# Splitting a parameter load, folding gates into small vectors and shifting with a second tensor, in a long convolution with a gated feed-forward

## The chip, the cores and the metric

The kernel runs on one core of a Trainium2 chip. The metric is the device time of one execution in microseconds, and less is better. The core's engines each work through a queue of their own in order: TensorE (PE in the profile, PEld for its weight loads), VectorE (DVE), ScalarE (ACT), GpSimd (POOL) and SyncE (SP), which issues most DMAs. TensorE writes to PSUM, which this kernel uses as eight banks of 128 x 512 float32. A "column" below is one element in each of 128 partitions.

## The reference

With L = 2048 tokens, D = 640 channels, N = 128 states per channel and F = 1728:

```python
mod = (silu(c) @ w_mod).reshape(1, 6, 1, 640)
sa, ca, ga, sb, cb, gb = (mod[:, i] for i in range(6))
h = layernorm(x) * (1 + ca) + sa
x = x + ga * A(h)
h = layernorm(x) * (1 + cb) + sb
x = x + gb * B(h)

# A(u): a long convolution, channel by channel
dt = exp(log_dt); A = -exp(log_A_real) + 1j * A_imag
C = (C_real + 1j * C_imag) * dt[:, None]
K[d, l] = 2 * Re(sum over n of C[d, n] * exp(A[d, n] * dt[d] * l))
y = irfft(rfft(u, 4096) * rfft(K, 4096))[:2048] + u * D_skip

# B(x): a gated feed-forward
out = (silu(x @ w1) * (x @ w3)) @ w2
```

All is float32.

## The kernel before, in words

The program has two parts. The first, up to about 376 us of the span, is A with the first layer norm; the second is B. The change is in the first.

**Blocks and chunks.** A goes through the 640 channels in five blocks of 128 (b = 0 to 4). The kernel K of a block is generated in eight chunks of 16 channels (`gen_chunk`): POOL adds two tables of phases into `ph` (`g*.ph` in the plan) and multiplies two tables of magnitudes into `yy` and `xx` (`z0` to `z2`), ScalarE takes sines of `ph` into PSUM (`s0` to `s4`, tile `tr`), VectorE multiplies them with the magnitudes (`m0` to `m4`), PE contracts over the states into `kps` (`p`), and ScalarE copies the result into `ks` (`r`). The tokens of the block go another way: they are normalized into a PSUM bank (`h*.n`, tile `hn`), multiplied by the row `rA` (`h*.x`), `rB` is added (`h*.a`, tile `hb`), and they go through DRAM into `xb`. Both then pass a two-stage Fourier transform on PE (tiles `ps`, then `fh` and `fk`), a product on VectorE (`fp`), an inverse stage (`fz`) and a store (`zd`).

**Tables.** For each half block, `tables` makes the phase tables `p1` (eight entries) and `p2` (four) from a start `pB` and a step `pS`, which are integers whose overflow is the wrap of the angle. Doublings of the step (times 1, 2, 4, 8, 16) are made first, then sums fill the tables. For the first half of block 0 VectorE makes the doublings by five shifts; for the other nine POOL makes them by a copy and four additions of a number to itself (tiles `p` and `step`).

**Gates.** `row` makes the first three rows of mod on PE; ScalarE copies them into `m`, PE spreads them over the partitions (`prow`), ScalarE copies them into `rows`, and `fold` on VectorE makes rA = (1 + ca) ga and rB = sa ga, 640 columns each. So the gate ga is applied to the tokens ahead of the convolution.

**Parameters.** The four parameter arrays of all blocks are loaded as 128 x 640, one DMA each, ahead of the tokens `xs`. `param_steps` then works on them: the turning angles for all five blocks at once (`pa`), the magnitudes and angles of C for block 0 and for the rest apart (`pb`, `pc`), and PE turns the results so that states lie on partitions (`ptp`).

**Order.** The 1,507 tasks of this part are added to a `Plan` with engines and dependencies, and they are issued in the order that the table `ORDER` gives; a letter behind a number chooses the engine where there are two (`a` ScalarE, `d` VectorE, `p` POOL). Each engine keeps that order. A wait at the head of a queue thus holds up all behind it. Nearly all instructions are recorded under one helper line (L146 before, L147 after), so the tile's name tells them apart.

**PSUM.** Three banks are for `tr`, one for `kps`, and four for everything else. `pbank` hands these four out in turn: three in a ring with the tag `f`, and each fourth request gets the one with the tag `x`. Some early tasks take only from the ring.

Of the kernel before, what the change touches and what calls it, by code (L numbers as in the profile page):

```python
# [10 lines left out]
F32 = mybir.dt.float32  # L11
F32R = mybir.dt.float32r
I32 = mybir.dt.int32
# [5 lines left out]
P = 128  # L19
# [9 lines left out]

EXPS = ((0, 0, 0, 64.0), (0, 1, 0, 1.0), (1, 0, 0, 512.0), (1, 1, 4, 8.0), (1, 2, 0, 8.0))  # L30
# [4 lines left out]
1 2 3 78 4 80 5 6 81 19 14 82 20 41 84 21 7 15 83 42 8 22 153d 9 13 16 154 43 17 23 10 44 24 18 93 25 28 45 89 59 30 26 29 46 31  # L35
35 91 39 47 27 48 87 96 49 36 100 33 156 61 98 50 109 37 157 34 60 107 32 158 105 111 51 102 113 95 52 88 104 90 53 62 108 72 74
70 76 38 40 159p 160 155d 85 161 103 162 114 116 54 115 170 55 174 117 186 97 118 94 119 171 79 112 86 120 56 99 172 57 121 175
179 187 176 313 58 177 180 173 64 106 182 190 188 11 67 298 181 178 189 191 183 122 66 192 196 308 65 193 202 197 195 194 184 68
110 303 199 63 101 123 206 203 69 71 92 138 419d 207 12 185 124 208 140 198 205 142 127 204 125 200 209 163 128 420 218 132 166d
213 164 144 212 221 211 421d 214 165 167 219 168 169 75 73 77 126 134 135 129 130 133 139 210 314d 222 131 309a 227 141 136 304a  # L40
215 234 310 216 315 223 311 224 220 143 316 312 217 237 305 299a 339 228 422 306 229 335 307 225 146 226 317 238 145 231 235 201
300 336a 250 239 230 337 240 245 232 241 301 236 242 243 302 233 251 148d 247 341 244 254 253 338d 255 246 252 256 147 266 342a
260 248 149 259 257 318 261 150 258 425d 262 267 249 270 343 340a 269 151 263 271 275 268 264 272 277 282 276 273 265 278 274
345 344a 426 279 286 283 287 346a 423 291 288 284 427 424 285 428 152 0 564 569 319 565d 321 320a 289 333 570a 292 579 566 280
294 334a 322a 829 567 436 327 290 293 281 571 331 328a 295 440 437 137 580d 347 441 439 332a 442 572 296 574 438 447 443 452 445
325 444 581 297 348a 568 446 329 326a 449 455 456 448 349 457 453 458 463 450 684p 350d 330a 830d 459 323 451 460 454 582 834
# [1849 lines left out]
```

## Time and profile before

| | us |
|---|---|
| median of three runs | 946.7 |
| lowest, highest | 944.83, 949.02 |
| profiled execution, its own time | 945.42 |
| its span, first to last instruction | 943.6 |

The mean granted clock of TensorE was 0.986. Over the whole span PE is busy for 848.8 us (90%), VectorE for 699.6 (74%), ScalarE for 524.2 (56%), POOL for 341.3 (36%). These shares mix two parts with different limits, so tables by stage are read instead. A row of a group gives engine, operation, output<-inputs, shape and count, then busy time, mean duration of one in ns, and the idle time of the engine just before. In a timeline the columns are start, length, engine, operation and, in brackets, idle time and what ended it. A row of waits gives who waited for whom, the total, how often, and the longest.

### The profile page before, as it was taken

To read this page: it belongs to the slowest core of one execution; us is meant where nothing else is said; L and a number is where in the kernel's file an instruction comes from. 1 tells how busy PE (TensorE), PEld (TensorE's weight loads), DVE (VectorE), ACT (ScalarE), POOL (GpSimd) and SP (SyncE) were. 2 spreads that over 40 slices of the span, in tenths; PEclk is the share of its full clock that TensorE was granted. 3 is DMA by queue.
4 is the path that set the end of the run, shared out by engine and by line. 5 is a ranking of instruction groups with operands and counts; after the bars stand their busy time and mean duration, and the time that the engine had idled before them with its cause. 6 is when DMAs were issued, how large, how long until landed. Compare 5 with 4: busy or idle time off the path is not lost.

```text
span 943.6 us, 21995 instructions
## 1 busy us (share of the span) xinstructions
PE 848.8 (90%) x8963; PEld 671.7 (71%) x8963; DVE 699.6 (74%) x1223; ACT 524.2 (56%) x900; POOL 341.3 (36%) x352
## 2 busy tenths in 40 slices
PE   1167788989989997999999999999999999999997
PEld 0035767767868752777877788888888888888875
DVE  7999999989999855467567576467568777765763
ACT  6898999989788842333333244344344434445331
POOL 1888999988999533000000000001133322200000
PEclk9998999999999997999999999999999999999999
DMA  9776554433223468965515262322132111123242
GB/s 210 236 255 166 169 139 121 105 103 92 59 71 89 130 187 238 235 176 158 157 55 150 84 166 79 112 84 71 36 79 81 51 44 48 41 83 112 74 152 82
DMA packets 124940, 112.77 MB, mean 120 GB/s; under 512 B 12328, under 2 KB 107048, under 8 KB 123560
## 3 DMA queue, kind: packets, MB, share of 16 engines
q1 hardware_dynamic: 124072, 110.46, 42.1%
q8 instruction: 70, 1.15, 0.5%
q10 hardware_dynamic: 768, 0.92, 0.4%
q14 instruction: 30, 0.25, 0.1%
HBM read 90.38 MB, written 20.97 MB: 118 GB/s over the span
## 4 chain that ended last, share of the span: by engine, by line
PE 65%; DVE 17%; ACT 7%; DMA 6%; issue 3%; POOL 1%; SPq 1%; DVEq 0%; ACTq 0%; POOLq 0%
PE p L819 17%; PE acc L1066 17%; PE gu L1029 7%; PE gu L1031 6%; PE gu L1030 6%; DVE yy L146 5%; DVE fp L146 3%; DVE xx L146 2%; DMA xs<-in_x 2%; ACT tr L146 2%; PE fz L146 2%; PE kps L146 2%; PE ps L146 2%; DVE fk L146 1%; PE fk L146 1%
## 5 line engine op out<-in xcount | busy, mean ns | idle before, releaser
L1029 PE MATMUL gu<-xh,wh 128*128 128x512 f32 x270 | 106.1, 398 | 1.6 <-ACT xh L608 1.4
L1031 PE MATMUL gu<-xh,wl 128*128 128x512 f32 x270 | 105.4, 390 | 0.0
L1030 PE MATMUL gu<-xl,wh 128*128 128x512 f32 x270 | 105.2, 389 | 0.0
L146 ACT ACTIVATE tr<-ph 128x512 f32<-128x512 int32 (+1 forms) x160 | 93.6, 601 | 11.4 <-DVE yy L146 6.9
L838 POOL TENSOR_TENSOR ws<-wp 128x256 f32<-128x256 f32 x13 | 9.6, 739 | 230.9 <-DVE x L609 116.0
L146 POOL TENSOR_TENSOR ph<-p,p 128x1024 int32<-128x1024 int32 x40 | 79.1, 1979 | 11.4 <-ACT tr L146 8.6
L146 DVE TENSOR_TENSOR yy<-yy,tr 128x512 f32<-128x512 f32 (+1 forms) x80 | 75.1, 942 | 1.1
L722 ACT ACTIVATE wh<-wr 128x640 fp32r<-128x640 f32 x51 | 35.0, 732 | 67.8 <-PE gu L1030 58.3
L819 PE MATMUL p<-x,wch 128*128 128x512 f32 x208 | 68.3, 389 | 0.0
L1029 PEld LDWEIGHTS gu<-xh,wh 128*128 128x128 f32 x270 | 50.6, 188 | 17.6 <-DVE al L609 2.1
L1031 PEld LDWEIGHTS gu<-xh,wl 128*128 128x128 f32 x270 | 50.7, 188 | 11.2 <-DVE wl L732 0.4
L146 PE MATMUL kps<-yy,xx 128*32 128x64 f32 x2560 | 48.7, 226 | 10.9 <-DVE xx L146 6.4
L1030 PEld LDWEIGHTS gu<-xl,wh 128*128 128x128 f32 x270 | 50.7, 188 | 10.2 <-DVE xl L609 0.2
L735 POOL MEMSET w2l<- 64x640 f32 x1 | 0.6, 627 | 157.1 <-PE acc L1066 157.1
L146 DVE TENSOR_TENSOR xx<-tr,xx 128x512 f32<-128x512 f32 x80 | 54.2, 679 | 1.2 <-ACT tr L146 0.7
L856 DVE TENSOR_TENSOR s<-p,s 128x512 f32<-128x512 f32 x52 | 34.7, 683 | 26.8 <-ACT s L854 22.8
L146 POOL TENSOR_TENSOR yy<-e,e 128x512 f32<-128x512 f32 x48 | 52.9, 1110 | 3.3 <-issue 1.7
L1042 ACT ACTIVATE th<-gu 128x512 f32<-128x512 f32 x26 | 15.6, 600 | 65.7 <-PE gu L1031 65.7
L146 PE MATMUL ps<-wk,xb 128*64 128x128 f32 x640 | 47.7, 297 | 4.9 <-DVE hb L146 1.9
L1044 DVE TENSOR_TENSOR a<-a,gu 128x512 f32<-128x512 f32 x26 | 17.9, 687 | 45.4 <-PE gu L1031 45.2
L146 PEld LDWEIGHTS kps<-yy,xx 128*32 128x32 f32 x2560 | 42.9, 112 | 11.7 <-issue 8.5
L146 PEld LDWEIGHTS ps<-wk,xb 128*64 128x64 f32 x640 | 42.9, 220 | 10.4 <-DVE hb L146 2.2
(378 smaller groups left out, 2378.9 us busy)
## 6 DMA issues: line engine op xcount, KB each, us to landing
wr<-in_w SPq DMA_DIRECT2D x52, 320.0 KB, 3.6
zd<-zt SPq DMA_DIRECT2D x39, 256.0 KB, 4.1
w2r<-in_w SPq DMA_DIRECT2D x26, 320.0 KB, 3.5
wp<-in_w SPq DMA_DIRECT2D x26, 320.0 KB, 3.6
wq<-in_w SPq DMA_DIRECT2D x26, 320.0 KB, 3.3
low<-zd SPq DMA_DIRECT2D x48, 160.0 KB, 5.5
xs<-in_x SPq DMA_DIRECT2D x16, 320.0 KB, 11.3
hs<-hb SPq DMA_DIRECT2D x20, 256.0 KB, 3.1
```

The lines of the kernel that those rows point to most:

```text
L146: self.prev = self.k.order(f(*a, **kw), self.prev)
L722: self.nc.scalar.activation(wh[:, i], raw[:, i], AF.Copy)
L735: self.nc.gpsimd.memset(w2l[64:].bitcast(F32), 0.0)
L819: nc.tensor.matmul(to, t[:, o], y[:, k], start=start and k == i == 0, stop=stop and (k, i) == (n - 1, 2), skip_group_check=True)
L838: G.tensor_tensor(s[0], a21, a22, op=ALU.add)
L856: add = lambda o, bk, s: V.tensor_tensor(o, bk, s, op=ALU.add)
L1029: nc.tensor.matmul(pg, wh[:, k, :], xh[:, k, :], start=(k == 0), stop=False)
L1030: nc.tensor.matmul(pg, wh[:, k, :], xl[:, k, :], start=False, stop=False)
L1031: nc.tensor.matmul(pg, wl[:, k, :], xh[:, k, :], start=False, stop=(k == KT - 1))
L1042: nc.scalar.activation(th, gu[0], AF.Tanh, scale=0.5)
L1044: nc.vector.tensor_mul(a, a, gu[1])
L1066: nc.tensor.matmul(acc[k], *two(a, w), start=(m == 0 and i == 0), stop=(m == 12 and i == 2))
```

## The change

Five edits come at once, with a new `ORDER` of 1,500 tasks.

1. Loads. Block 0's parameters are loaded first by four DMAs of 128 x 128, the rest behind by four of 128 x 512. The turning angles, the exponential of log_A and its product with dt are worked for block 0 and for the rest apart.
2. Gates. The rows of mod are turned onto partitions by PE into a bank (`vp`), and eight small VectorE instructions (`vc`) make A = (1 + ca) ga and B = sa / (1 + ca) there, with block 0's B multiplied by its A. PE spreads A and B over the partitions. Only block 0's tokens are still multiplied by rA. For blocks 1 to 4 A goes into the magnitudes of K (`gm`, four POOL instructions) and into D_skip (`gd`, four), and `h*.x` is gone.
3. Tables. For every half block VectorE makes all five doublings in one `tensor_tensor` shift of 128 x 640, whose second input is a tensor of amounts. POOL keeps four sums per table.
4. Banks. The four banks have names. In running the order, `Plan.run` gives each request the bank whose last release stands earliest in the order.
5. The tiles `ph`, `xx` and `yy` are allocated by their own tasks, and the magnitudes (`z`) no longer follow `ph` in the plan.

```diff
+SHIFTS = 0, 1, 3, 2, 4
...
-        def begin(e):
-            by = by_t(pS)
-            to = (p1[:, :, :, 1], by_t(st[:, 0]), by_t(st[:, 1]), p2[:, :, :, 1], by_t(st[:, 2]))
-            for i, d in enumerate(to):
-                if e == "DVE":
-                    V.tensor_scalar(d, by, i, None, op0=ALU.logical_shift_left)
-                elif i:
-                    add(d, to[i - 1], to[i - 1])
-                else:
-                    G.tensor_copy(d, by)
+        def begin():
+            sh = self.shifts
+            amounts = bass.AP(tensor=sh.tensor, offset=sh.offset, ap=[list(sh.ap[0]), [0, HB2], [0, 2], list(sh.ap[1])])
+            V.tensor_tensor(p1[:, :, :, 1:6], bc(by_t(pS), 3, 5), amounts, op=ALU.logical_shift_left)
...
+        def bank(key):
+            free = [-1 if k is None else max((at.get(x, 1e9) for x in self.gives.get(k, [])), default=1e9) for k in held]
+            i = free.index(min(free))
+            held[i] = key
+            return i
...
     def pbank(self, name):
-        self.banks += 1
-        if self.banks % 4 == 3:
-            return self.psx.tile([P, 512], F32, name=name, tag="x")
-        return self.psg.tile([P, 512], F32, name=name, tag="f", bufs=3)
+        return self.psg.tile([P, 512], F32, name=name, tag=f"b{self.plan.banks.pop(0)}", bufs=1)
...
-            add(n + "x", "DVE", .61, lambda i=i: self.h_mul(b, i), [n + "n", "fold"], t + .1)
+            if b == 0:
+                add(n + "x", "DVE", .61, lambda i=i: self.h_mul(b, i), [n + "n"] + rows, t + .1)
...
-        add("T", "SP", 0, lambda: self.param_load(T, slice(0, NB)), [], next(lp), dma=[327680] * 3)
+        add("T0", "SP", 0, lambda: self.param_load(T, one), [], next(lp), dma=[65536] * 3)
+        def load_rest():
+            nc.sync.dma_start(self.la[:, 1:], self.log_ar.rearrange("(k p) n -> p k n", p=P)[:, 1:])
+            self.param_load(T, rest)
...
+        def gates():
+            pv = mt[1]
+            sa, ca, ga = (pv[:, k * KT:k * KT + KT] for k in range(3))
+            z, A, B, q = pv[:, 16:16 + KT], ab[:, :KT], ab[:, KT:2 * KT], ab[:, 2 * KT:]
+            V.tensor_scalar(q, ca, 1.0, None, op0=ALU.add)
+            V.scalar_tensor_tensor(z, q, -1.0, q, op0=ALU.mult, op1=ALU.max)
+            V.tensor_scalar(z, z, 1e-18, 4e-18, op0=ALU.is_lt, op1=ALU.mult)
+            V.tensor_tensor(q, z, q, op=ALU.add)
+            V.tensor_mul(A, q, ga)
+            V.reciprocal(q, q)
+            V.tensor_mul(B, sa, q)
+            V.tensor_mul(B[:, :1], B[:, :1], A[:, :1])
...
-        def fold():
-            self.rA, self.rB = self.rows[1], self.rows[0]
-            V.scalar_tensor_tensor(self.rA, self.rA, 1.0, self.rows[2], op0=ALU.add, op1=ALU.mult)
-            V.tensor_mul(self.rB, self.rB, self.rows[2])
+        def gate_sizes(e):
+            m = self.mag[:, 1:].rearrange("p b (e j) -> p b e j", j=4)
+            r = self.rA[:, P:].rearrange("p (b j e) -> p b e j", j=4, e=E4)
+            for k in range(NB - 1):
+                self.eng(e).tensor_tensor(m[:, k], m[:, k], r[:, k], op=ALU.mult)
```

Where instructions moved is seen best at three places. The first is the start of VectorE's queue, behind the instructions on dt (`st_n`); `wb` holds exp(log_A), `x_e` the imaginary parts and C, `xb` and `ks` scratch. Before:

```order
L146 TENSOR_TENSOR wb<-wb,st_n_95 128x640
L146 TENSOR_TENSOR x_e<-x_e,st_n_95 128x640
L146 TENSOR_TENSOR xb<-x_e 128x128
L146 TENSOR_SCALAR ks_134<-x_e 128x640
L146 TENSOR_SCALAR xb<-xb 128x128
L146 TENSOR_TENSOR ks_133<-al,j_109 128x1024
```

Now:

```order
L147 TENSOR_TENSOR xb<-x_e 128x128
L147 TENSOR_TENSOR x_e<-x_e,st_n_92 128x128
L147 TENSOR_SCALAR xb<-xb 128x128
L147 TENSOR_SCALAR ks_136<-x_e 128x128
L147 TENSOR_TENSOR wb<-wb,st_n_92 128x128
L147 RECIPROCAL xb<-xb 128x128
L147 TENSOR_TENSOR ks_135<-al,j_106 128x1024
L147 TENSOR_TENSOR x_e<-x_e,st_n_92 128x512
```

Seven instructions on block 0 now stand ahead of the first one that needs the rest of the parameters.

The second place is the table of the second half of block 2. On POOL before (`p_123` is `p1`, `p_124` is `p2`):

```order
L146 COPY p_123<-pS 128x128
L146 TENSOR_TENSOR step<-p_123 128x64x2
L146 TENSOR_TENSOR step<-step 128x64x2
L146 TENSOR_TENSOR p_124<-step 128x128
L146 TENSOR_TENSOR step<-p_124 128x64x2
L146 TENSOR_TENSOR yy_2029<-e_121,e_122 128x16x32
L146 TENSOR_TENSOR xx_2028<-e_121,e_122 128x512
L146 TENSOR_TENSOR yy_2029<-e_121,e_122 128x16x32
L146 TENSOR_TENSOR ph_2169<-p_118,p_119 128x1024
L146 TENSOR_TENSOR p_123<-p_123,step 128x128x2
```

On POOL now (`p_120` and `p_121`):

```order
L147 COPY p_121<-pB 128x128
L147 TENSOR_TENSOR ph_2097<-p_115,p_116 128x1024
L147 TENSOR_TENSOR yy_2151<-e_118,e_119 128x16x32 x2
L147 TENSOR_TENSOR p_121<-p_121,p_120 128x128
L147 TENSOR_TENSOR xx_2202<-e_118,e_119 128x512
L147 TENSOR_TENSOR ph_2211<-p_115,p_116 128x1024
L147 TENSOR_TENSOR yy_2267<-e_118,e_119 128x16x32 x2
L147 TENSOR_TENSOR p_121<-p_121,p_120 128x128x2
```

and on VectorE now, where the shift stands:

```order
L147 TENSOR_TENSOR xx_1946<-tr_224_1976,xx_1946 128x512
L147 TENSOR_TENSOR yy_1930<-yy_1930,tr_224_1949 128x16x32
L147 TENSOR_TENSOR p_120<-pS,shifts 128x128x5
L147 TENSOR_TENSOR hb_2044<-hn,rw 128x512
L147 SCALAR_TENSOR_TENSOR yy_1930<-yy_1930,tr_224_1949 128x16x32
```

The doublings have gone from five POOL instructions to one of VectorE's, which stands between products of chunks and the sum for `hb`; no `hn<-hn,rw` stands ahead of that sum any more.

The third place is the end of the last chunk in VectorE's queue (`xx` is a chunk's last product, `sp<-ps` empties a bank of the kernel's first transform stage, `fp` is the product of spectra). Before:

```order
L146 TENSOR_TENSOR xx_4832<-tr_608_5121,xx_4832 128x512
L146 TENSOR_TENSOR xx_4832<-tr_608_5188,xx_4832 128x512
L146 TENSOR_TENSOR fp_5321<-fk_5303,hq 128x2x2x128
L146 TENSOR_TENSOR fk_5303<-fk_5303,hq 128x512
L146 TENSOR_TENSOR fp_5321<-fp_5321,fk_5303 128x256 x2
```

Now:

```order
L147 TENSOR_TENSOR xx_4956<-tr_608_5115,xx_4956 128x512
L147 COPY sp<-ps_5023 128x16x2x16
L147 COPY sp<-ps_5204 128x16x2x16
L147 COPY sp<-ps_5203 128x16x2x16
L147 COPY sp<-ps_5239 128x16x2x16
L147 TENSOR_TENSOR fp_5300<-fk_5282,hq 128x2x2x128
```

Two of PE's four groups of that stage now stand behind the last chunk, where one stood before (the other group is the one whose bank is `ps_5239`), and four evictions on VectorE stand ahead of the first spectrum product.

More of the change, by code (lines that the diff above doesn't have):

```diff
@@ L181, in add @@
         self.tasks[name] = (eng, f, tuple(after))
+        self.takes[name] = [name + "'" * i for i, x in enumerate(take) if x[0] == "bank"]
+        for tag, key in give:
+            if tag == "bank":
+                self.gives.setdefault(key, []).append(name)
     def run(self):
         T = list(self.tasks.items())
-        done = set()
+        done, at, held = set(), {}, [None] * 4
+        def bank(key):
+            free = [-1 if k is None else max((at.get(x, 1e9) for x in self.gives.get(k, [])), default=1e9) for k in held]
+            i = free.index(min(free))
+            assert free[i] < 1e9, key
+            held[i] = key
+            return i
         for x in ORDER.split():
@@ L190, in run @@
             done.add(n)
+            at[n] = len(at)
+            self.banks = [bank(k) for k in self.takes[n]]
             if f:
@@ L1483, in first_tasks @@
         for i in range(8):
-            bank = "f2" if b == 0 and m and i < 6 else "bank"
-            later = [f"k0.{x}.m" for x in range(6)] + ["colsf"]
+            bank = "bank"
             t = W[g](b, i)
@@ L1786, in rows_begin, with turn_cols @@
             A.activation(m[:96, 384:], pm[0][:96, 384:], AF.Copy)
-        add("m", "ACT", .9, rows_begin, ["mr4"], 20, take=[("hz", 4)], give=[("x", "mr0")])
+        add("m", "ACT", .9, rows_begin, ["mr4"], 20, take=[("hz", 4)], give=[("bank", "mr0")])
+        ab = e.tile([P, 3 * KT], F32, name="ab")
+        def turn_cols():
+            pv = mt[1] = self.pbank("pvm")
+            for o in range(4):
+                nc.tensor.matmul(pv[:, o:16:4], mt[0][:, o * P:(o + 1) * P], self.ident[:, 0:P:32], start=True, stop=True)
@@ L1795, in keep @@
+        self.rA, self.rB = self.rw[:, 1], self.rw[:, 0]
         def keep(g):
[L1796 to L1803 removed]
@@ new lines, in early_tasks @@
+        for g in range(3):
+            add(f"pr{g}", "PE", .9, lambda g=g: spread(g), ["vc"], 21, take=[("bank", 1)])
+            add(f"rw{g}", "ACT", .5, lambda g=g: keep(g), [f"pr{g}", "lat1", "pa1.4"], 21, give=[("bank", f"pr{g}")])
+        rows = [f"rw{g}" for g in range(3)]
+        def gate_sizes(e):
[3 more added lines that the diff above has]
+                self.eng(e).tensor_tensor(m[:, k], m[:, k], r[:, k], op=ALU.mult)
@@ new lines, in gate_skip @@
+        def gate_skip(e):
+            for q in range(4):
+                s = slice(32 * q, 32 * q + 32)
+                d = self.dsk[s, 1:]
+                self.eng(e).tensor_tensor(d, d, self.rA[s, P:].rearrange("p (b q e) -> p b q e", q=4, e=E4)[:, :, q], op=ALU.mult)
+        add("gm", ("POOL", "DVE"), (1.5, 1.0), gate_sizes, ["q1.v3"] + rows, 22, port=True)
+        add("gd", ("POOL", "DVE"), (1.5, 1.0), gate_skip, ["dsk"] + rows, 22, port=True)
+        add("wb", "SP", 0, lambda: nc.sync.dma_start(self.wb, self.t_wb), rows + ["mr4", "lat1", "turn1"], 60, dma=[2097152])
```

290 lines of the change are left out of this document (148 added, 142 removed).

## The prediction

> **What bounds the kernel now.** I read the busy time by stage first. The columns are PE, PEld, DVE, ACT and POOL busy time, the granted clock and the DMA.
>
> ```profile
> core 0: us, PE busy (x) PEld busy (x) DVE busy (x) ACT busy (x) POOL busy (x), PEclk, DMA share, GB/s
> 20.00:80.00 60.00, 26.35 (x342) 14.07 (x342) 57.66 (x111) 52.82 (x107) 45.22 (x44) 0.91 0.71 221
> 80.00:200.00 120.00, 99.58 (x2445) 84.36 (x2442) 115.12 (x193) 113.07 (x209) 115.70 (x116) 0.99 0.51 135
> 200.00:332.00 132.00, 123.91 (x3236) 100.23 (x3240) 121.84 (x200) 111.91 (x199) 111.47 (x104) 1.00 0.34 95
> 332.00:376.00 44.00, 36.13 (x311) 18.45 (x300) 26.26 (x75) 13.22 (x22) 16.14 (x14) 0.88 0.76 212
> 376.00:943.00 567.00, 559.72 (x2638) 452.50 (x2638) 365.17 (x614) 222.05 (x348) 51.04 (x57) 1.00 0.36 101
> ```
>
> From 376 us on the feed-forward part runs, with PE busy for 559.72 of 567 us. The change touches nothing there, so I carry those 567 us over. The change lives in the first 376 us, the convolution. There VectorE is the fullest engine from 20 us on: 57.66 of 60, 115.12 of 120, 121.84 of 132. From 80 to 332 us it is idle for 252 - 236.96 = 15.0 us. POOL is as full up to 200 us, and PE is fuller than VectorE after 200 us (123.91 of 132). So I count VectorE's queue to the last chunk of generated kernel and ask what its idle time does; PE after 200 us is the limit to watch.
>
> Then the waits from 80 to 332 us, VectorE's first (total, times, longest):
>
> ```profile
> DVE sp L146 <- PE ps L146: 3.7, 4, 1.3
> DVE fp L146 <- PE fk L146: 3.2, 4, 0.9
> DVE yy L146 <- POOL yy L146: 0.2, 1, 0.2
> ```
>
> and PE's:
>
> ```profile
> PE fh L146 <- ACT hq L146: 2.1, 4, 0.8
> PE fh L146 <- DVE fp L146: 2.0, 3, 1.1
> PE ps L146 <- DVE fp L146: 1.9, 2, 1.4
> PE ps L146 <- ACT hq L146: 1.7, 2, 1.0
> ```
>
> VectorE waits 6.9 us for PE in these rows and 0.2 us for POOL: a lighter POOL does not free VectorE directly. The PE rows are waits for a PSUM bank, since hq and fp are no inputs of ps or fh; only the engine that empties the bank ties them. They sum to 7.7 us.
>
> **The change part by part.** *Start.* VectorE's queue and SP's, with the idle time in brackets:
>
> ```profile
> 6.16 0.82 DVE L146 TENSOR_TENSOR wb<-wb,st_n 128x640 f32<-128x640 f32 x1
> 9.94 0.82 DVE L146 TENSOR_TENSOR x_e<-x_e,st_n 128x640 f32<-128x640 f32 x1 [2.97 <-DMA x_e<-in_a_im]
> ```
>
> ```profile
> 3.52 0.78 SPq L146 DMA_DIRECT2D x_e<-in_a_im  x1
> 4.34 2.81 SPq L146 DMA_DIRECT2D xs<-in_x  x5
> ```
>
> Today VectorE idles 2.97 us until the whole of A_imag has landed. With block 0 loaded apart, a fifth of the bytes is enough, and the small instructions on block 0 can run in that time. But four more DMAs go into SP's queue ahead of the x loads, at 2.81/5 = 0.56 us each, so the other four blocks land no earlier than today, and VectorE may run dry again before they do. The ends are 0 and -3.0; nothing in the rows lies nearer to one of them, and I take the middle, -1.5 us. VectorE has a backlog from here to 332 us, so the gain is kept. The x loads are issued 2.2 us later, but they queue on full DMA engines anyway.
>
> *VectorE's queue up to the last chunk.* Rows of the groups, 0 to 332 us:
>
> ```profile
> L146 DVE TENSOR_TENSOR hn<-hn,rw 128x512 f32<-128x512 f32 x20 | 13.7, 688 | 1.5 <-ACT hn L146 1.5
> L146 DVE SCALAR_TENSOR_TENSOR rw<-rw,wb 128x640 f32<-128x640 f32 x1 | 2.4, 2352 | 0.0
> L146 DVE TENSOR_TENSOR rw<-rw,wb 128x640 f32<-128x640 f32 x1 | 1.7, 1679 | 0.0
> L146 DVE TENSOR_TENSOR wb<-wb,st_n 128x640 f32<-128x640 f32 x1 | 0.8, 818 | 0.0
> L146 DVE SCALAR_TENSOR_TENSOR rs_n_h<-st_n,rs_y_h 128x16 f32<-128x16 f32 x1 | 1.7, 1656 | 0.0
> L146 DVE TENSOR_TENSOR rsw<-rsw,rs_w_h 128x16 f32<-128x16 f32 x3 | 0.5, 182 | 0.1
> L146 DVE TENSOR_TENSOR e<-e,mag 128x512 f32<-128x512 f32 x2 | 3.8, 1898 | 0.0
> L146 DVE TENSOR_TENSOR x_e<-x_e,mag 128x512 f32<-128x512 f32 x1 | 0.7, 679 | 0.0
> L146 DVE TENSOR_TENSOR xs_al<-al,j 128x1024 f32<-128x1024 f32 x1 | 1.2, 1219 | 0.0
> L146 DVE TENSOR_SCALAR p<-pB 128x128 int32<-128x128 int32 x3 | 2.5, 842 | 0.0
> L146 DVE TENSOR_SCALAR step<-pS 128x128 int32<-128x128 int32 x3 | 0.7, 277 | 0.0
> ```
>
> In a full queue an instruction starts 0.08 us before the one ahead of it ends, so a 688 ns multiply costs 0.61. Sixteen of the twenty multiplies by the gate row go: -9.8. The fold (2.35 + 1.68, less overlap) goes: -3.9. The gates' eight small instructions on 128x5 come: eight at 0.21 (182 ns and the step to the next), and for the two that read SBUF twice a short wait: +2.5, with 1.7 and 4.1 as ends. The parameter steps in two pieces are six more instructions at the fixed part of one, which lies between 0.08 (182 ns for 16 columns, less the overlap) and 0.2: +0.8.
>
> The new shift is the disputed price. It has 640 elements per partition, as has the 818 ns row, so 0.74 in the queue, against five short ones in one of ten tables and none in nine. Yet VectorE's instructions whose tensors all lie in SBUF take much longer in the middle of POOL's work than alone: the fold's 2352 and 1679 against 818, 1656 against 182 for 16 columns, 1898 against 679, 842 against 277. Timeline, VectorE and POOL at 225 us:
>
> ```profile
> 225.41 1.96 DVE L146 TENSOR_TENSOR e<-e,mag 128x512 f32<-128x512 f32 x1
> ```
>
> ```profile
> 224.88 1.94 POOL L146 TENSOR_TENSOR ph<-p,p 128x1024 int32<-128x1024 int32 x1
> 226.78 0.86 POOL L146 TENSOR_TENSOR p<-p 128x128 int32<-128x128 int32 x1
> ```
>
> The product began behind ph and ended when ph's end (226.82) plus its own 0.6 had passed; POOL's next one then took 0.86, where other sums of 128 columns take 0.43 (the rows below). The shift reads pS and the amounts from SBUF, so it waits for POOL in the same way. The rows above give the waits of ten instructions: 1.53, 0.86, 1.47, 1.22 twice, 0.57 on average for the three p copies, and 0 twice (x_e<-x_e,mag; xs_al, whose 1219 ns are what 1024 columns cost at 679 for 512): 8.0 us, 0.80 each. POOL's share from 80 to 332 us falls from 90% to some 82% (below), which brings 0.74. So 1.48 per shift: nine new ones are +13.3. Ends: no wait, +6.7; the rest of a whole ph each time (1.95), +24.2. I take the middle since that is where the rows lie.
>
> [...]
>
> By choices of engine that stand in the new order, VectorE loses one product with j (-1.1), one of three products with mag (-1.5 on average), one p copy (-0.8) and one eviction of 512 columns (-0.6), and gains one normalization of four times 128 columns (between four times 0.28 and 0.6, I take +1.6): -2.4. Sum: -9.8 - 3.9 + 2.5 + 0.8 + 13.3 - 2.4 = +0.5 us. VectorE's queue stays as long as it was.
>
> Behind a shift on VectorE stand the products yy and xx and the sum hb; ScalarE's sines wait for the former's PSUM and SP's stores for the latter. That wait is in the 0.74.
>
> *POOL.* The steps that it loses, and those that change:
>
> ```profile
> L146 POOL COPY p<-pS 128x128 int32<-128x128 int32 x9 | 3.9, 433 | 0.0
> L146 POOL TENSOR_TENSOR step<-p 128x128 int32<-128x128 int32 x18 | 7.8, 435 | 1.4
> L146 POOL TENSOR_TENSOR p<-step 128x128 int32<-128x128 int32 x9 | 3.9, 433 | 0.7
> L146 POOL TENSOR_TENSOR step<-step 128x128 int32<-128x128 int32 x9 | 3.8, 423 | 0.7
> L146 POOL TENSOR_TENSOR p<-p,step 128x256 int32<-128x256 int32 x20 | 18.3, 913 | 4.7 <-DVE step L146 4.6
> L146 POOL TENSOR_TENSOR p<-p,step 128x512 int32<-128x512 int32 x10 | 13.4, 1336 | 0.0
> ```
>
> The first four rows go: 19.4 busy and 2.8 idle between. Per table two sums of 256 columns, one of 512 and one of 128 (0.43) become two of 128, one of 256 and one of 384 (between, 1.1): 3.6 to 2.9, so -7. The gates on magnitudes and skip are eight instructions of 0.43, +3.4. Three tasks given to it, of 1024, 512 and 128 columns, bring +3.3 at ph's rate. That is -22, some 20 of it from 80 to 332 us. POOL also blocks nine times for 0.74 behind a shift. VectorE waited for it 0.2 us, so the sum books nothing here.
>
> *Banks.* A task now takes the bank whose release stands earliest in the order, not the next in a ring of three with every fourth task on the other. Of PE's 7.7 us of bank waits and of VectorE's 6.9 us behind PE, which overlap, I take half of the latter: -3.5, with 0 and -6.9 as ends, since no row tells whether another bank was free.
>
> *Tail.* PE after the last chunk:
>
> ```profile
> 331.20 1.16 PE L146 MATMUL ps<-wk,ks 64*64 64x64 f32 x64 [0.48 <-ACT ks L146]
> 332.29 1.13 PE L146 MATMUL fh<-sp,wb 128*64 128x128 f32 x16
> 333.56 2.98 PE L146 MATMUL fk<-sp,wb 128*64 128x128 f32 x48
> ```
>
> In the new order two ps groups stand there instead of one, and the fh between them and fk has gone ahead: +1.16, less the fh that covered the eviction: +0.5, between -1 and +2.
>
> Sum: -1.5 + 0.5 - 3.5 + 0.5 = -4.0 us on the profiled execution's 945.42 us (span 943.6, 1.8 around it): 941.4. The median of the runs, 946.7, lies 1.3 above it, so 942.7.
>
> **The rivals.** *PE sets the second half.* For it: 123.91 of 132 us, and PE's work is the same. Against: VectorE's waits for PE are matched by PE's for VectorE and ScalarE. The bank term falls away: -0.5, so 946.2.
>
> [...] If a shift waits 0.2 us instead of 0.74, VectorE's queue gets 4.9 shorter, and with the other half of its waits for PE the sum is -12.4: 934.3. For it: waits of 0 occur in the rows (679). Against: POOL stays over 80% full.
>
> *The shifts wait for whole instructions (slower).* Place: nine shifts, several next to a ph. At 1.95 us each instead of 0.74 VectorE's queue grows by 10.9, sum +6.9, so 953.6. It decides from 0.74 + 4.0/9 = 1.2 us of wait per shift, where the gain is gone. For it: 1.22 twice and 1.53. Against: three rows near 0.5 and two at 0. [...]
>
> *The shift does not run at one element per cycle.* If its repeated amounts double it to 1.48 us: +6.7 on the sum, so 949.4. No row shows such an operand in a shift.
>
> **How the numbers follow.** Forecast 0.40, with its own range 938.5 to 946; PE 0.21; ports free 0.20; whole waits 0.13; slow shift 0.06. Leaving out most of the whole waits and the lower part of the free ports gives 933.5 to 951. What a measurement can tell from no change is 0.5%, 4.7 us: under 942.0 lie the free ports (0.20), a little under half of the forecast (0.18) and the lower end of the PE case (0.03), 0.41; above 951.4 most of the whole waits and some of the slow shift, 0.13; the rest 0.46.
>
> **What would show it.** Right: VectorE's first long gap under 2 us; shifts of p from pS at 0.8 to 2 us, on average near 1.5; no hn<-hn,rw after block 0; VectorE's busy time from 20 to 332 us within 3 us of 294.6; POOL's 20 us lower; fewer waits of ps and fh for hq and fp. Wrong: shifts near 0.8, or above 2; the last xx product later than 329.4 us; or new waits of POOL's p sums for the shift, or of VectorE for POOL's ph.

## The result and the profile after

| | us |
|---|---|
| before, median of five runs (lowest, highest) | 946.7 (944.83, 949.02) |
| changed, median of five runs (lowest, highest) | 940.27 (938.05, 941.85) |
| profiled executions, before and changed | 945.42 and 938.05 |
| ratio changed / before, 95% interval | 0.9928 (0.9905 to 0.995) |

The kernel is faster by 0.72%, 6.8 us by the ratio and 6.4 by the medians. The forecast was 942.7, or -4.0. The traces below are of one execution each, and the changed kernel's is the fastest of its five, 2.2 us under their median. Where the time went shows first in two places of the timeline. VectorE's last product of generated kernel, xx, of before (the second of the two) and of the changed kernel:

```profile
327.94 1.48 DVE L146 TENSOR_TENSOR xx<-tr,xx 128x512 f32<-128x512 f32 x2
```

```profile
317.39 0.68 DVE L147 TENSOR_TENSOR xx<-tr,xx 128x512 f32<-128x512 f32 x1
```

It ends at 329.4 before and at 318.1 after, so the generation is 11.3 us shorter. The first product of the feed-forward part, before and after:

```profile
376.19 0.98 PE L1029 MATMUL gu<-xh,wh 128*128 128x512 f32 x3 [1.41 <-ACT xh L608]
```

```profile
365.31 0.98 PE L1044 MATMUL gu<-xh,wh 128*128 128x512 f32 x3 [1.40 <-ACT xh L623]
```

10.9 us are still there. The spans end 7.3 us apart (943.6 and 936.3), so 3.6 us are given back in a part that nobody changed. They go at two places, 1.3 and 2.3 us. The first is a wait of PE near 395 us for a normalized tile that stands behind a late weight load (ScalarE waits 9.0 us for `wr`, VectorE behind it 8.3); before, the same product did not wait:

```profile
PE gu L1044 <- DVE x L609: 1.1, 1, 1.1
```

The second is the last 70 us, where VectorE waits longer for the weights `wq`; before (876 to 922 us) and after (868 to 914):

```profile
DVE wq L1013 <- DMA wq<-in_w: 7.9, 7, 2.6
```

```profile
DVE wq L1028 <- DMA wq<-in_w: 12.4, 7, 3.6
```

Now the stages of the changed kernel, with the columns as in the prediction (PE, PEld, DVE, ACT, POOL, clock, DMA):

```profile
20.00:80.00 60.00, 25.36 (x354) 15.26 (x356) 54.58 (x113) 50.92 (x102) 40.01 (x39) 0.87 0.79 236
80.00:200.00 120.00, 107.34 (x2616) 90.71 (x2616) 118.28 (x198) 116.47 (x216) 113.43 (x101) 1.00 0.52 139
200.00:332.00 132.00, 124.71 (x3196) 101.57 (x3196) 120.68 (x204) 105.51 (x189) 105.01 (x93) 0.99 0.36 97
```

Look at the second row. From 80 to 200 us VectorE is idle for 1.7 us (before 4.9), ScalarE for 3.5 (6.9), POOL for 6.6 (4.3). Three engines that need one another are full at the same time, more evenly than before. VectorE's busy time from 20 to 332 us is 293.5 (forecast: within 3 of 294.6); POOL's is 258.5, down 13.9 from 272.4 (forecast: 20 lower). But equal windows do not hold equal work here: this one now takes in 14 us behind the last xx, before it took in 2.6. Counted from the start of the span to the end of the last xx, VectorE's work fell from 308.2 to 300.3 us and POOL's from 274.1 to 258.0.

From 104 us to the last xx the sums of the stretches are, before and after:

```profile
sum 225.40, PE 202.80 PEld 166.20 DVE 213.37 ACT 201.49 POOL 203.17; mean PE 28.97 PEld 23.74 DVE 30.48 ACT 28.78 POOL 29.02
```

```profile
sum 214.10, PE 200.21 PEld 165.21 DVE 206.94 ACT 196.51 POOL 191.41; mean PE 28.60 PEld 23.60 DVE 29.56 ACT 28.07 POOL 27.34
```

VectorE has 6.4 us less to do and idles 7.2 us instead of 12.0. At 104 us the changed kernel is not ahead by the count of products: the sixteenth xx ends at 104.0, before at 101.3 (the twentieth at 113.3, before at 114.9). Over the whole way to the last xx VectorE has 7.8 us less to do and idles 17.8 us instead of 21.3; the two make the 11.3. VectorE's waits from 80 to 332 us, and PE's for banks that are being emptied into hq and fp:

```profile
DVE sp L147 <- PE ps L147: 4.9, 5, 3.0
DVE fp L147 <- PE fk L147: 2.6, 2, 1.3
DVE yy L147 <- ACT tr L147: 2.5, 2, 2.3
DVE xx L147 <- ACT tr L147: 1.9, 4, 0.7
```

```profile
PE ps L147 <- ACT hq L147: 1.0, 1, 1.0
PE fk L147 <- DVE fp L147: 1.2, 1, 1.2
PE fk L147 <- ACT hq L147: 0.5, 1, 0.5
PE ps L147 <- DVE fp L147: 0.2, 1, 0.2
```

Those of ps and fh, which the prediction added up, fall from 7.7 to 1.2 us, as the forecast had it (with those of fk, from 8.9 to 2.9); VectorE's waits for PE do not fall with them (7.5 us in the first two rows, 6.9 before). The disputed shift, and the multiplies that stayed for block 0:

```profile
L147 DVE TENSOR_TENSOR p<-pS,shifts 128x640 int32<-128x640 int32 x10 | 9.9, 988 | 0.0
L147 DVE TENSOR_TENSOR hn<-hn,rw 128x512 f32<-128x512 f32 x4 | 2.8, 694 | 0.1
```

The row of 640 columns that the prediction started from took 818 ns; against it the ten shifts took 0.17 us more each, not 0.74. Six took 0.82 to 0.84 us, and four of these began with POOL idle. The other four, of 0.95 to 1.66 us, began while an instruction of POOL's ran and ended 0.68 or 0.69 us after its end. The longest, with POOL's instructions around it:

```profile
94.60 1.66 DVE L147 TENSOR_TENSOR p<-pS,shifts 128x640 int32<-128x640 int32 x1
```

```profile
94.49 1.08 POOL L147 TENSOR_TENSOR xx<-e,e 128x512 f32<-128x512 f32 x1
95.51 1.67 POOL L147 TENSOR_TENSOR yy<-e,e 128x512 f32<-128x512 f32 x1
```

POOL's next one took longer as well, here 1.67 us where the mean of its yy<-e,e is 1.11. VectorE's first long gap is 0.79 us instead of 2.97:

```profile
10.19 0.69 DVE L147 TENSOR_TENSOR x_e<-x_e,st_n 128x512 f32<-128x512 f32 x1 [0.79 <-DMA x_e<-in_a_im]
```

Of the signs that the prediction named, the short first gap, the missing multiplies and the shorter waits of ps and fh came. The shifts did not come as forecast: six of the ten take 0.82 to 0.84 us and the average is 0.99, not 1.5, which is nearer to the sign of being wrong, "shifts near 0.8". POOL's sums for the tables also wait 12.6 us for the shift, 11.1 of it once at the start, where they waited 4.6 for the doublings. Whether the reasons hold needs the parts one by one.

### The profile page after: what moved, and what is told of

Its sections match the earlier page's. It is cut to its first block, busy times and chain, and to the rows that moved or that the text cites. A ratio compares the mean times of both kernels' runs of the same rounds, so it can differ in the third digit from the quotient of the medians.

```text
span 936.3 us, 21994 instructions
## 1 busy us (share of the span) xinstructions
PE 846.5 (90%) x8983; PEld 673.8 (72%) x8983; DVE 693.9 (74%) x1228; ACT 518.7 (55%) x892; POOL 325.2 (35%) x323
## 4 chain that ended last, share of the span: by engine, by line
PE 64%; DVE 8%; ACT 8%; DMA 7%; issue 3%; SPq 0%; POOL 0%; DVEq 0%; ACTq 0%
PE p L834 17%; PE acc L1081 16%; PE gu L1044 6%; PE gu L1046 6%; PE gu L1045 6%; PE ps L147 4%; ACT tr L147 2%; PE fz L147 2%; DMA low<-zd 2%; DVE fp L147 2%; DVE yy L147 2%; PE kps L147 2%; DMA wq<-in_w 2%; PE fk L147 1%; DMA x<-in_x 1%
## 5 line engine op out<-in xcount | busy, mean ns | idle before, releaser
L147 ACT ACTIVATE tr<-ph 128x512 f32<-128x512 f32 (+1 forms) x160 | 93.8, 603 | 8.8 <-POOL ph L147 3.9
L147 DVE TENSOR_TENSOR xx<-tr,xx 128x512 f32<-128x512 f32 x80 | 54.3, 683 | 2.0 <-ACT tr L147 1.9
L147 PE MATMUL fh<-sp,wb 128*64 128x128 f32 x640 | 45.2, 286 | 6.3 <-issue 2.2
```

The costliest lines, as they stand in the source:

```text
L147: self.prev = self.k.order(f(*a, **kw), self.prev)
```

## The experiments

Three theories. **A**, the prediction's: VectorE's queue sets the time, and what is added to it or taken from it counts in full, while POOL's load costs nothing. **B**: POOL sets the time, so the gain comes from the doublings that it lost. **C**, formed after the first four runs: no engine alone sets it. The order was written for the loads of three engines that are all nearly full; what is added to one costs about its length or more, what is taken from one brings little, and a gain needs an order made for the new loads.

All kernels were timed in rounds with the kernel before. "Against its base" is the difference of ratios times 946.7 us, the base being the changed kernel (0.9928) for the new order and the kernel before (1) for the old. The loads in the names are as planned; by the busy times of the traces they are 18.7 us on POOL in e3, and 9.2 and 8.6 on VectorE in e4 and e6.

| run | ratio to before, 95% | against its base, us |
|---|---|---|
| e1 new order, doublings on POOL again | 1.003 (1.0018 to 1.0042) | +9.7 |
| e2 new order, shifts twice | 1.0063 (1.0047 to 1.0078) | +12.8 |
| e3 new order, POOL +19.4 us | 1.0094 (1.0068 to 1.012) | +15.7 |
| e4 new order, multiplies kept | 1.0088 (1.0069 to 1.0106) | +15.1 |
| e9 new order, banks released last | 1.0075 (1.0051 to 1.0099) | +13.9 |
| e10 new order, one load | 0.9934 (0.9919 to 0.995) | +0.6 |
| e11 new order, POOL -13.5 us | 0.9949 (0.9932 to 0.9966) | +2.0 |
| e12 new order, two moves | 0.9941 (0.9919 to 0.9963) | +1.2 |
| e5 old order, shift | 1.0095 (1.0072 to 1.0117) | +9.0 |
| e6 old order, no multiplies | 0.9988 (0.9975 to 1.0) | -1.1 |
| e7 old order, banks | 1.0 (0.9987 to 1.0014) | 0.0 |
| e8 old order, all three | 1.0023 (1.001 to 1.0036) | +2.2 |

**e1, the doublings on POOL again.**

```diff
-        return [("DVE", .75, begin),
+        def double():
+            G.tensor_copy(p1[:, :, :, 1], by_t(pS))
+            for i, j in ((2, 1), (4, 2), (3, 4), (5, 3)):
+                add(p1[:, :, :, i], p1[:, :, :, j], p1[:, :, :, j])
+        return [("DVE", .75, begin) if b == h == 0 else ("POOL", 1.9, double),
```

> Nine of the ten shifts on VectorE become a copy and four sums of 128 columns on POOL at the same places in the order; everything else is the changed kernel (940.3). Theory A, VectorE's queue sets the end of the convolution and POOL does not: VectorE loses 9 x (0.99 - 0.08) = 8.2 us, POOL gains 9 x 5 x 0.43 = 19.4 us that cost nothing, so about 932 (930 to 936). Theory B, the lighter POOL brought the gain: POOL is as full as in the kernel before, and the time goes back to some 945 to 952.

Measured: 948.66 us, as B has it; 8.2 us less on VectorE brought nothing. VectorE now waits for POOL, which it hardly did in either kernel, and ScalarE waits for it longer than in the changed kernel (3.9 us there; 20 to 330 us):

```profile
DVE yy L147 <- POOL yy L147: 6.3, 8, 1.9
```

```profile
ACT tr L147 <- POOL ph L147: 7.9, 11, 1.7
```

**e2, each shift twice.**

```diff
-            V.tensor_tensor(p1[:, :, :, 1:6], bc(by_t(pS), 3, 5), amounts, op=ALU.logical_shift_left)
+            for _ in range(2):
+                V.tensor_tensor(p1[:, :, :, 1:6], bc(by_t(pS), 3, 5), amounts, op=ALU.logical_shift_left)
```

> Each of the ten shifts is issued twice, with the same result. Theory A: ten more instructions in VectorE's queue at 0.74 (no wait for POOL) to 0.91 us (the average measured in the changed kernel, 0.99 less 0.08), +7.4 to +9.1, so 947.7 to 949.4. Theory B: POOL has room behind the shift that it did not have before, and VectorE waits for others anyway, so +0 to +3, 940 to 943. If the second of two shifts waits for a whole instruction of POOL, a mean of over 1.5 us shows in the group of the shifts.

Measured: 952.22 us. The group of the shifts:

```profile
L147 DVE TENSOR_TENSOR p<-pS,shifts 128x640 int32<-128x640 int32 x20 | 21.8, 1092 | 0.3
```

That is 11.9 us more than the 9.9 of the changed kernel, or 11.1 in the queue with 0.08 us less for each of the ten, by which the next instruction starts before a shift ends (in the changed kernel's trace at 33.50 us, behind the shift of 0.82 that starts at 32.76). The time grew by 12.8: VectorE's additions count in full. B alone, which allowed 3, is out.

**e3, POOL's load alone.**

```diff
+        def more():
+            add(p2[:, :, :, 1], p2[:, :, :, 0], p1[:, :, :, 3])
+            if b or h:
+                for i in range(5):
+                    add(self.junk[:, i % 2], self.junk[:, 1 - i % 2], self.junk[:, 1 - i % 2])
```

> Five sums of 128 columns on scratch tiles are added on POOL to each of nine tables, 19.4 us in all, as much as the doublings that POOL lost; VectorE's instructions are those of the changed kernel. Theory A: POOL's load alone costs nothing, 940 to 943 (the shifts and other instructions of VectorE with two inputs in SBUF wait a little more often). Theory B: the time follows POOL, +8 to +19, so 948 to 959.

Measured: 956.96 us, B's number. A, by which POOL's load costs nothing, is out. The way to VectorE goes by ScalarE's sines, which wait for ph, and by yy itself (20 to 330 us):

```profile
ACT tr L147 <- POOL ph L147: 10.7, 9, 2.5
```

```profile
DVE yy L147 <- POOL yy L147: 6.4, 6, 1.7
```

VectorE's own work up to the last xx grew by 4.0 us as well, 2.8 of them in longer shifts (1.26 us on average, in the changed kernel 0.99).

**e4, the multiplies kept.**

```diff
     def h_add(self, pc, b):
+        if b:
+            self.h_mul(pc, b)
         x = self.xq.pop((pc, b))
```

> The sixteen multiplies of the rows of blocks 1 to 4 by the gate row are put back on VectorE ahead of the sums that form hb, while the gates stay folded, so the gate is applied twice. Theory A: sixteen times 0.61 us in VectorE's queue, +9.8, so 950. Theory B, the multiplies were hidden in VectorE's waits: +0 to +4, 940 to 944.

Measured: 954.81 us, +15.1 for 9.8 us of work, half as much again as A allowed. The stage from 80 to 200 us:

```profile
80.00:200.00 120.00, 98.62 (x2334) 83.81 (x2334) 114.24 (x189) 106.06 (x192) 102.01 (x90) 0.94 0.50 129
```

VectorE, ScalarE and POOL are idle for 5.8, 13.9 and 18.0 us, against 1.7, 3.5 and 6.6 in the changed kernel. A multiply that comes late holds up the sums and products behind it in VectorE's queue, ScalarE's sines and POOL's ph wait for those, and each wait holds up the rest of that engine's queue: the three wait for one another in turn. That is a reading of the idle times; no single row shows the chain. This profiled execution is the slowest of the six (958.33), the granted clock of the stage is 0.94 against 1.00, and PE has more of the stops of the last section (6.2 us against 3.3), so what the excess over 9.8 us is made of is not shown. C was formed here.

**e5, the shift in the old order.**

```diff
+        if b or h:
...
+                V.tensor_tensor(p1[:, :, :, 1:6], bc(by_t(pS), 3, 5), amounts, op=ALU.logical_shift_left)
+            steps = [first,
+                     lambda e: add(p2[:, :, :, 1], p2[:, :, :, 0], p1[:, :, :, 3]),
+                     lambda e: add(p2[:, :, :, 2:4], p2[:, :, :, 0:2], bc(p1[:, :, :, 5], 3, 2)),
+                     lambda e: add(p1[:, :, :, 3], p1[:, :, :, 1], p1[:, :, :, 2]),
+                     lambda e: add(p1[:, :, :, 5:8], p1[:, :, :, 1:4], bc(p1[:, :, :, 4], 3, 3))]
+            go = lambda e="POOL": steps.pop(0)(e)
+            return [("DVE", .75, shift), ("POOL", .4, go), ("POOL", .4, go), (("DVE", "POOL"), (.15, .28), go), ("POOL", .8, go), ("POOL", 1.1, go)]
```

> The kernel before (946.0) with its old order, in which nine tables are doubled by the shift on VectorE and finished by the four sums on POOL, in the places of the old six steps. VectorE gets 9 x 0.91 = +8.2 us, POOL loses 19.4 us of doublings and some 6 us of sums. Theory A, VectorE's queue sets the time: 952 to 954. Theory B, POOL sets it: 932 to 940. Theory C, no engine alone sets it, since the order was fitted to the loads of three engines that are all nearly full, so that what is added costs and what is taken from one engine brings little: 946 to 954.

Measured: 955.58 us. Less work on POOL (322.8 us over the whole span, before 341.3, so 18.5 less and not the 25 expected) brought nothing; nine shifts of 1.23 us (10.4 in the queue) cost 9.0.

```profile
L146 DVE TENSOR_TENSOR p<-pS,shifts 128x640 int32<-128x640 int32 x9 | 11.1, 1232 | 0.0
```

B is out for the kernel before; A and C both fit. VectorE's whole work up to the last xx grew by 5.4 us only, since others of its instructions became shorter or fell away. The shift by itself makes the kernel slower by 0.95%.

**e6, the multiplies left out of the old order.**

```diff
-            add(n + "x", "DVE", .61, lambda i=i: self.h_mul(b, i), [n + "n", "fold"], t + .1)
+            add(n + "x", "DVE", .61, None if b else lambda i=i: self.h_mul(b, i), [n + "n", "fold"], t + .1)
```

> The kernel before without the sixteen multiplies by the gate row of blocks 1 to 4 (the gate is left out of their data); nothing takes their place. VectorE loses 9.8 us. Theory A: 936 to 937. Theory B: 945 to 946. Theory C: a part of it, as far as VectorE was the last of the three, 940 to 945.

Measured: 944.63 us, -1.1 by the ratio for 9.8 us less. From 80 to 200 us:

```profile
80.00:200.00 120.00, 102.49 (x2462) 86.55 (x2463) 109.50 (x181) 114.25 (x213) 117.34 (x116) 0.99 0.52 139
```

VectorE has become idle (10.5 us instead of 4.9), POOL is down to 2.7 and ScalarE to 5.8. VectorE's waits of 80 to 332 us, where in the kernel before it waited 3.2 and 3.7 us for PE (fp and sp) and not at all for ScalarE's sines:

```profile
DVE fp L146 <- PE fk L146: 5.0, 6, 1.6
DVE sp L146 <- PE ps L146: 4.4, 4, 2.1
DVE yy L146 <- ACT tr L146: 3.5, 6, 1.3
DVE xx L146 <- ACT tr L146: 1.9, 3, 0.9
```

The work went and waits took its place.

**e7, the banks in the old order.**

```diff
-        self.banks += 1
-        if self.banks % 4 == 3:
-            return self.psx.tile([P, 512], F32, name=name, tag="x")
-        return self.psg.tile([P, 512], F32, name=name, tag="f", bufs=3)
+        return self.psg.tile([P, 512], F32, name=name, tag=f"b{self.plan.banks.pop(0)}", bufs=1)
```

> The kernel before with its old order, but each task of PE takes the one of the four PSUM banks whose release stands earliest in the order, as in the changed kernel. The working of the prediction gives -3.5 (0 to -6.9), so 942.5 (939 to 946). If the banks only matter together with an order that was made for them, 945 to 947.

Measured: 946.75 us, ratio 1.0. The choice by earliest release is worth nothing to the old order.

**e8, the three together in the old order** (the edits of e5, e6 and e7).

> The three edits of the last runs together in the old order: shift and four sums, no multiplies (the gates of blocks 1 to 4 are left out), banks by earliest release. VectorE -1.6 us, POOL -25 us. If the parts alone make the gain, this has to be at or under the changed kernel, 935 to 940. If the gain is made by the order that was written for the new loads, 942 to 948.

Measured: 948.66 us. The kernel is 9.0 us slower than the changed one (0.0095 of 946.7), and no faster than the kernel before. A stage, and the last product xx (the second of the two):

```profile
80.00:200.00 120.00, 100.56 (x2442) 84.75 (x2441) 110.41 (x181) 111.93 (x208) 104.37 (x93) 0.97 0.50 134
```

```profile
328.31 1.48 DVE L146 TENSOR_TENSOR xx<-tr,xx 128x512 f32<-128x512 f32 x2
```

From 80 to 200 us the three are idle for 9.6, 8.1 and 15.6 us: none is full. POOL waits 13.3 us for ScalarE before its ph (80 to 332 us):

```profile
POOL ph L146 <- ACT tr L146: 13.3, 8, 3.2
```

The busy times from the start of the span to the end of the last xx, in us:

| | VectorE | ScalarE | POOL | end of the last xx |
|---|---|---|---|---|
| before | 308.2 | 287.4 | 274.1 | 329.4 |
| e8 | 303.9 | 286.9 | 254.5 | 329.8 |
| changed | 300.3 | 282.4 | 258.0 | 318.1 |

Against the kernel before, VectorE has 4.3 us less to do and POOL 19.5 less, and the generation ends no earlier. This is the run on which the explanation rests: the parts alone bring nothing in the old order. Against the changed kernel the generation ends 11.7 us later; 3.6 of that is work of VectorE, and 8.1 is time in which it idles. Part of the load differs too: the new order gives some evictions and normalizations of ScalarE's to VectorE, and e8 has neither the split load, nor the gates in small vectors, nor the tiles that are allocated by their own tasks. Of these only the load was tried alone (e10). So the 9.0 us are the worth of the order together with the choices of engine and the allocation that it uses.

**e9, banks chosen badly in the new order.**

```diff
-            i = free.index(min(free))
+            i = max((x, k) for k, x in enumerate(free) if x < 1e9)[1]
```

> The changed kernel (940.3) with its order, but each task of PE takes, of the banks that are free in the order, the one released last instead of the one released first; 183 of 238 choices come out another way. Theory C, the order was made for its banks as for its loads: PE waits for hq, fp, sp and the like again, 950 to 965. If banks hardly matter, as in the old order (946.75 against 946.26), 940 to 942.

Measured: 953.13 us, +13.9. VectorE and PE wait again (80 to 332 us):

```profile
DVE sp L147 <- PE ps L147: 6.7, 4, 4.9
DVE fp L147 <- PE fk L147: 4.0, 7, 1.8
```

```profile
PE ps L147 <- ACT sp L147: 4.2, 5, 1.2
```

The banks are a part of what the order was written for: nothing by themselves, much inside it. In this trace the last xx ends 6.7 us later than in the changed kernel and the feed-forward part begins 13.8 later, so half of the loss stands behind the generated chunks.

**e10, one load of the parameters.**

```diff
-        add("T0", "SP", 0, lambda: self.param_load(T, one), [], next(lp), dma=[65536] * 3)
-        add("T1", "SP", 0, load_rest, [], next(lp), dma=[262144] * 4)
+        def load_all():
+            nc.sync.dma_start(self.la[:, 1:], self.log_ar.rearrange("(k p) n -> p k n", p=P)[:, 1:])
+            self.param_load(T, slice(0, NB))
+        add("T0", "SP", 0, lambda: load_all(), [], next(lp), dma=[65536] * 3)
+        add("T1", "SP", 0, None, [], next(lp), dma=[262144] * 4)
```

> The changed kernel with the parameters of all five blocks loaded in one, ahead of block 0's steps, which stay apart from the others'. VectorE's first long gap is 0.79 us in the changed kernel and should be near 3 again. The working of the prediction gives +1.5 (0 to +3), 941.8. Theory C with another stage as the limit of the start (the x loads and the means and squares on ScalarE): 0 to +0.5, 940 to 941.

Measured: 941.3 us, +0.6 and not to be told from nothing (the two intervals leave some 2.6 us either way). VectorE's start:

```profile
9.29 0.29 DVE L147 TENSOR_TENSOR xb<-x_e 128x128 f32<-128x128 f32 x1 [3.02 <-ACT x_e L147]
10.38 0.29 DVE L147 TENSOR_TENSOR x_e<-x_e,st_n 128x128 f32<-128x128 f32 x1 [0.79 <-DMA x_e<-in_a_im]
```

The gap is back, 3.8 us in two pieces instead of 0.79, and the sixteenth product xx ends at 104.2 us instead of 104.0. Nearly all of the gain of the start is used up before then. (This profiled execution is the slowest of its seven, 945.14 us.)

**e11, POOL relieved in the new order.**

```diff
-            G.memset(p1[:, :, :, 0], 0)
+            G.memset(p1, 0)
...
-                ("POOL", .4, lambda: add(p1[:, :, :, 3], p1[:, :, :, 1], p1[:, :, :, 2])),
-                ("POOL", 1.1, lambda: add(p1[:, :, :, 5:8], p1[:, :, :, 1:4], bc(p1[:, :, :, 4], 3, 3)))]
+                ("POOL", .4, (lambda: add(p1[:, :, :, 3], p1[:, :, :, 1], p1[:, :, :, 2])) if b == h == 0 else None),
+                ("POOL", 1.1, (lambda: add(p1[:, :, :, 5:8], p1[:, :, :, 1:4], bc(p1[:, :, :, 4], 3, 3))) if b == h == 0 else None)]
```

> The changed kernel without the last two sums on POOL of nine tables (they are left out, so parts of the tables keep old values): POOL has 9 x 1.5 = 13.5 us less to do, nothing else changes. Theory B, POOL sets the time: 928 to 933. Theory C, what is taken from one engine alone brings little: 937 to 940.

Measured: 942.13 us, +2.0, which the intervals do not tell from nothing. POOL's work fell by 11.7 us in all, since clearing the two tables whole at the start takes 1.7 us more, and the time shows no gain, not even C's small one. In the trace there is one and it is lost again: the last xx ends at 316.2 us, 1.8 earlier than in the changed kernel, but the feed-forward part begins at 368.9, 3.6 later. POOL waits for ScalarE instead (it was 2.8 us), and VectorE and ScalarE stay as full as they were:

```profile
80.00:200.00 120.00, 107.07 (x2672) 90.44 (x2670) 118.00 (x199) 116.67 (x218) 107.88 (x93) 1.00 0.52 137
```

```profile
POOL ph L147 <- ACT tr L147: 9.3, 8, 2.1
```

**e12, two moves in the order.** In the table, 1195 (the eviction w3.6.h) goes behind 1234 (g4.0.s2); 1398 (k4.2) goes ahead of 1338 (g4.6.p) and its evictions 1399 and 1400 just behind that, and 1445 and 1446 (w4.5) go behind k4.3.

> The changed kernel with two moves in the order and no change in any load: ScalarE's eviction w3.6.h, for which ScalarE waits 2.65 us and VectorE behind it 2.27 us, goes behind the first sines of block 4's first chunk, and the product k4.2 with its two evictions goes ahead of the last generated chunk, where the tail now waits for it. Theory C: -1 to -3, 937 to 939.5. If the order is as good as any near it, 940 to 942.

Measured: 941.14 us, no gain; this miss of C says that a wait seen in the trace is not yet a fault of the order. VectorE's wait at that place stayed, 2.99 us instead of 2.27, and ScalarE's moved from the eviction to the next thing that needed PE:

```profile
272.11 1.22 DVE L147 TENSOR_TENSOR yy<-yy,tr 128x1024 f32<-128x1024 f32 x1 [2.99 <-ACT tr L147]
```

```profile
270.71 0.38 ACT L147 ACTIVATE ks<-kps 128x256 f32<-128x256 f32 x1 [3.05 <-PE kps L147]
```

PE itself had stopped (last section). No run had a lower median than the changed kernel.

## Why the prediction was right, and which of its steps were not

The time fell inside the range, 2.4 us under the forecast. The reasons hold less well than the number, and that the number came so near is in part luck. In the two traces VectorE's work up to the last xx fell by 7.8 us where the sum had +0.5, and its idle time by 3.5; but 3.6 us were lost in the feed-forward part, which the sum carried over unchanged.

- **Start, -1.5.** The gap went as described. The step "VectorE has a backlog from here to 332 us, so the gain is kept" failed. With the load back (e10) the gap at the start is 3.0 us longer, and at 104 us 0.3 of that is left; the time, 0.6 us longer, could not tell 1.5 from nothing by itself. Against the kernel before, the sixteenth xx even ends 2.6 us later.
- **VectorE's queue, +0.5.** It became 7.8 us shorter. Of the 8.3 us between the two, nine shifts at 0.91 us in the queue instead of 1.48 make 5.1; the mis-sized term is the shift's wait, 0.17 us instead of 0.74. Another 2.1 us of work moved behind the last xx. The middle of ten other instructions' waits was taken, though the order could place each shift. In other runs a shift takes longer: 1.23 us on average in e5, 1.09 in e2, and the longest there 2.57 and 2.46. The rival that shifts wait for whole instructions of POOL needed 1.2 us of wait each; the longest shift of the changed kernel took 1.66 us, 0.84 over the 818 ns. So the rival with a wait of 0.2 us was half right, on the wait; its 934.3 was not reached. Its chance stands under the name of free ports, and no run shows ports: the traces show which shifts took longer, and what POOL did then.
- **POOL, 0.** "VectorE waited for it 0.2 us, so the sum books nothing here" holds for the saving alone: less work on POOL brought no gain in the old order (e5) nor in the new one (e11). It failed for the change as a whole, since the new order uses that room. With 19.4 us put back on POOL the kernel takes 15.7 us more (e3), and with the doublings back on POOL 9.7 more, though VectorE has less to do (e1). That a wait is absent from a trace shows that the engine keeps up, not that it has room: in the kernel before POOL was idle for 4.3 of 120 us.
- **Banks, -3.5.** The idle time of VectorE fell by 3.5 us and PE's waits of ps and fh for hq and fp by 6.5, close to the term, but not for its reason: the same choice of banks in the old order is worth 0.0 (e7), and VectorE's own waits for PE did not fall. In the new order a bad choice costs 13.9 us (e9).
- **Tail, +0.5.** The last eviction of block 4's ps ends at 324.5 us, before at 333.5: 9.0 earlier, where the last xx was 11.3 earlier, so the two ps groups took 2.3 us. Up to the first product of the feed-forward part all but 0.5 of that came back (47.2 us from the last xx on, before 46.8). The term is met in this trace only: in those of the other runs with the new order the stretch takes 48.2 to 54.3 us.
- **The sum.** Its form was wrong: it added savings on one queue. In the old order 9.8 us less on VectorE bring 1.1 (e6), and the three edits together lose 2.2 (e8), with 4.3 us less on VectorE and 19.5 less on POOL. What brought 0.72% is the order written for the new loads, with the choices of engine and the allocation that go with it: the same three edits without it are 9.0 us slower. The prediction took the new order into account only as a few choices of engine (-2.4).

Two things stay open. Which rows of the new order make the 9.0 us was not separated: with 1,500 numbers changed at once no single place was tried but the two of e12, and the allocation of ph, xx and yy was not tried alone. And why the last 70 us of the unchanged part wait longer for wq is not known. It goes with the new order: counted from 405 us on against the kernel before, the profiles of e1, e3, e10, e11 and e12 lose 2.4 to 3.4 us there, those of e5 and e7 none, and that of e8 1.4; no run tried it.

## What to carry to other kernels

Where three engines in a hand-written order are each idle for 1 to 6% of a stage, their loads cannot be priced one by one: here additions cost most of their length (15.7 us for some 19 on POOL) or more than it (15.1 for less than 10 on VectorE), and savings brought next to nothing until the order was written again. Try such a change in the old order and the old parts in the new one; the pair tells the worth of the order from that of the parts. A row with no wait for an engine is no proof that the engine has room; read its idle time too. And where a change moves the end of a stage, compare work up to the same instruction, not over equal windows.

## What the hardware showed

PE stops in the midst of groups of matmuls without a wait that the profile shows. The timeline of e10 shows four such stops in a row (the first begins before 265.86), each put down to "issue":

```profile
265.86 2.04 PE L147 MATMUL fh<-sp,wb 128*64 128x128 f32 x30 [1.47 <-issue]
267.83 0.24 PE L147 MATMUL kps<-dsk,ident 128*32 128x4 f32 x8
267.92 1.15 PE L147 MATMUL kps<-yy,xx 128*32 128x64 f32 x64
269.00 0.62 PE L147 MATMUL ps<-wk,ks 64*64 64x64 f32 x25
270.92 0.81 PE L147 MATMUL ps<-wk,ks 64*64 64x64 f32 x39 [1.30 <-issue]
271.65 1.99 PE L147 MATMUL fz<-fp,wz 64*128 64x512 f32 x8
273.57 1.16 PE L147 MATMUL ps<-wk,ks 64*64 64x64 f32 x64
274.66 0.24 PE L147 MATMUL kps<-dsk,ident 128*32 128x4 f32 x8
274.75 0.42 PE L147 MATMUL kps<-yy,xx 128*32 128x64 f32 x8
276.27 1.09 PE L147 MATMUL kps<-yy,xx 128*32 128x64 f32 x56 [1.11 <-issue]
277.30 1.16 PE L147 MATMUL ps<-wk,ks 64*64 64x64 f32 x64
278.39 0.75 PE L147 MATMUL ps<-wk,xb 128*64 128x128 f32 x7
280.27 0.92 PE L147 MATMUL ps<-wk,xb 128*64 128x128 f32 x11 [1.13 <-issue]
```

Count the matmuls between stops: 30 + 8 + 64 + 25 = 127, 39 + 8 + 64 + 8 + 8 = 127, 56 + 64 + 7 = 127. With a weight load each (the trace of the changed kernel has 8,983 of both) that is 254 instructions, and with the few others of PE's queue 255 or 256. The changed kernel, e10, e11 and e12 stop at the same matmul near 265 us, for 1.92, 1.47, 1.37 and 1.82 us; the place is fixed, the length is not. In the changed kernel ScalarE and VectorE wait 2.65 and 2.27 us behind that one, which is what e12 tried to mend in the order and could not.

The traces of all fourteen kernels show what the place is tied to. Number PE's queue through, with matmuls, weight loads and the sequencer's own instructions. From 80 to 330 us there are 51 stops of over 0.5 us that are put down to "issue", and 50 of them come at number 194 or 195 of a run of 256, in the old order and in the new. The changed kernel's three, at 214.94, 265.48 and 323.36 us, are at 194, 195 and 194; the one that does not fit is the kernel before's at 112.59 us, at number 32. In e4 and e9 PE's queue holds four more instructions of the sequencer than in the changed kernel, and stops come one or two matmuls earlier at the same numbers. So the stop goes with the number of the instruction and not with the work there. Between 1 and 7 of some 44 such places show one in each kernel, and the longest takes 2.6 us. They sum to 3.3 us in the trace of the changed kernel, to 5.9 in e2 and e3, 6.2 in e4 and 7.5 in e10; how much of the times of these runs they make was not separated.

What makes PE stop at these numbers was not shown: no row names a cause, and no run was made to test one. Most of the places show no stop of over 0.5 us.
